# Interleaving the first w_in matmuls with the last x matmuls of batch 0 in a fused attention and feed-forward kernel

## The chip, the cores and the metric

One core of one Trainium2 chip. The time is the device time of one execution in microseconds (us). The unchanged kernel takes 279.9 us (median of 3 runs, 279.63 to 279.91; with three more runs, taken for the result, the median is 279.63).

## The reference

```python
q_s = softmax(q, axis=-1)              # q, k, v: 8 batches, 8 heads, 576 rows, 64 columns
k_s = softmax(k, axis=2)
kv  = einsum('bhsd,bhse->bhde', k_s, v)
x   = einsum('bhsd,bhde->bhse', q_s, kv)   # then heads side by side: 4608 x 512
out = gelu(x @ w_in) @ w_out               # w_in 512 x 2048, w_out 2048 x 512
```

Below, "x of a pair" is x of two heads (128 of the 512 columns). x0 to x3 are the four pairs, and each is also one quarter of the contraction with w_in.

## The kernel before

TensorE works through the batches (512 of the 576 rows of each; the other 64 rows of all batches make a ninth round): kv, x, 64 w_in matmuls in 16 column tiles, and 64 w_out matmuls. Batch 0 is special, for nothing precedes it that could hide its waits. Its start (cuts marked with "..."):

```python
def kv_tiles(b):                       # PSUM for kv
    if b == 0:
        p = [psum_h.tile([128, 512], FP32, tag="h", name="kv")[:, 0:256] for i in range(2)]
        ps = psum_a.tile([128, 4, 256], FP32, tag="a2", name="kv")
        st[b]["kvall"] = ps[:, 0::2]
        p += [ps[:, 0, :], ps[:, 2, :]]
    ...
def kv_norm(b, half=None):             # reciprocal of a column, then a product, on VectorE
    ...
    elif b == 0 and half == 0:         # pairs 0 and 1: two times two instructions
        parts = [(st[b]["kv"][hp].unsqueeze(1), kvc[b][:, hp:hp + 1], 1) for hp in range(2)]
    elif b == 0:                       # pairs 2 and 3: two instructions for both
        parts = [(ps, kvc[b][:, 2:4], 2)]
...
kv_mm(0, 0)
kv_norm(0, 0)
tp_mm(0, 1)                            # transposes of q, second half
tp_evac(0, 1)
x_tile(0, 2, psum_a, "a")
x_mm(0, 0)                             # x0 and x1
x_evac(0, 0, "s")                      # "s": PSUM to SBUF on ScalarE; otherwise on VectorE
cast_wi_dm(0, wi[0], 0, nc.scalar)     # first piece of w_in (256 columns), first quarter
for dm in range(1, NDM):
    cast_wi_dm(0, wi[0], dm, nc.gpsimd)
kv_mm(0, 1)
kv_norm(0, 1)
x_evac(0, 1)
x_tile(0, 3, psum_h, "h")
x_mm(0, 1)                             # x2 and x3
x_evac(0, 2, "s")
x_evac(0, 3)
cast_wi(1, wi[1], "p")                 # second piece, on GpSimd
table(AF.Gelu)
...
h_phase(0, {0: [lambda: cast_wi(2, wi[2], "v")], ...}, groups={0: 2, 4: 4, 8: 4}, ...)
```

`groups={0: 2}` runs the first two tiles together: both tiles' matmuls on x0, then both on x1, on x2, on x3. This is eight matmuls; "the ninth" below is the first one of the third tile.

The softmax here doesn't subtract the row's maximum and nothing guards it: scores larger than these inputs give would overflow.

## Time and profile before

| | us |
|---|---|
| time, median of 3 | 279.9 |
| span in the profile | 278.0 |
| TensorE busy | 270.0 |
| longest wait of TensorE after its start | 0.61, at 13.4 us |
| first w_in matmul, ninth, first w_out matmul | 14.32, 16.06, 28.15 |

The profile's lines are in the prediction. A line of a timeline gives start, length, engine, line of the program, operation, tiles, shapes and count; in square brackets stands the idle time before it and what ended it. The kernel is bound by TensorE from about 10 us on; until then TensorE runs warm-up matmuls on zeros (8.55 of the first 10 us, counted as busy) while data arrive. A change at the start can gain or lose only by moving the moment from which TensorE runs without waits.

### The profile page before, as it was taken

The numbers are of one execution on the slowest core, as the hardware profiler recorded it, in microseconds if no ns is written. First come the engines' busy times: TensorE is split into PE (matmuls) and PEld (weight loads), VectorE is DVE, ScalarE is ACT, GpSimd is POOL, SyncE is SP. The second block draws the span as 40 slices with busy tenths as digits, with TensorE's granted clock in tenths as the row PEclk, the third lists the DMA queues.
The fourth block names the chain that finished last, engine by engine and source line by source line (L and its number), as shares of the span: only waits on it lengthen the run. The fifth ranks groups of instructions, "written<-read, shape, count | busy, mean of one in ns | idle before, by whom it ended". The sixth has DMA issues, their size and how long they took to land.

```text
span 278.0 us, 4534 instructions
## 1 busy us (share of the span) xinstructions
PE 270.0 (97%) x1891; PEld 126.5 (46%) x1919; DVE 100.7 (36%) x153; ACT 158.0 (57%) x247; POOL 32.8 (12%) x26
## 2 busy tenths in 40 slices
PE   7899999999999999999999999999999999999995
PEld 3444454444444444444444444444444444444443
DVE  2876574319743540093008400651015200130012
ACT  4867675789377816791569246943683363136400
POOL 1520051002020220014000500050005000000000
PEclk9999999999999999999999999999999999999999
DMA  7999999963993139702981199017502500220033
GB/s 253 398 386 429 397 402 407 398 257 103 287 348 61 66 79 295 283 38 86 267 329 40 42 247 383 38 51 190 115 0 75 151 2 0 75 78 0 0 78 77
DMA packets 44980, 50.10 MB, mean 180 GB/s; under 512 B 20384, under 2 KB 29856, under 8 KB 44704
## 3 DMA queue, kind: packets, MB, share of 16 engines
q1 hardware_dynamic: 44560, 49.39, 53.5%
q10 hardware_dynamic: 400, 0.43, 0.6%
q8 instruction: 15, 0.25, 0.3%
q14 instruction: 5, 0.04, 0.0%
HBM read 36.70 MB, written 9.44 MB: 166 GB/s over the span
## 4 chain that ended last, share of the span: by engine, by line
PE 94%; DMA 2%; issue 1%; ACT 1%; SPq 1%; DVE 0%
PE ps L327 44%; PE ps L355 43%; DMA f<-in_k_dram 2%; PE kv L199 2%; PE ps L294 2%; PE ps L380 1%; PE pair L327 1%; ACT ek L150 0%; ACT v_aug L160 0%; PE ps L255 0%; SPq L90 0%; PE ps L299 0%; SPq L103 0%; PE tp L255 0%; DVE kvc L218 0%
## 5 line engine op out<-in xcount | busy, mean ns | idle before, releaser
L327 PE MATMUL ps<-xT,wi_bf 128*128 128x512 bf16 x557 | 124.2, 380 | 0.5
L355 PE MATMUL ps<-wo_bf,g 128*128 128x512 bf16 x543 | 122.1, 380 | 1.6 <-issue 1.1
L333 ACT ACTIVATE g<-ps 128x512 bf16<-128x512 f32 x142 | 83.5, 598 | 66.8 <-PE ps L327 66.8
L327 PEld LDWEIGHTS <-wi_bf 128*128 128x128 bf16 x576 | 56.1, 98 | 68.0 <-issue 0.5
L355 PEld LDWEIGHTS <-g 128*128 128x128 bf16 x560 | 53.9, 98 | 64.3 <-issue 0.4
L363 DVE COPY y_sb<-ps 128x512 f32<-128x512 f32 x33 | 22.7, 687 | 81.7 <-PE ps L355 78.6
L238 POOL TENSOR_TENSOR e<-e,recq 128x2048 bf16<-128x2048 bf16 (+1 forms) x9 | 25.7, 2855 | 176.2 <-DVE recq L237 141.5
L162 DVE CAST v_aug<-f 128x576 bf16<-128x576 f32 x24 | 16.4, 746 | 47.5 <-DMA f<-in_v_dram 47.5
L236 DVE TENSOR_REDUCE qsum<-e 128x16 f32<-128x1024 bf16 (+1 forms) x13 | 21.1, 1621 | 14.4 <-ACT e L145 14.3
L320 ACT CAST xT<-ps 128x512 bf16<-128x512 f32 x18 | 9.9, 588 | 28.8 <-PE ps L294 18.8
L145 ACT ACTIVATE e<-f 128x512 bf16<-128x512 f32 (+1 forms) x42 | 20.5, 556 | 3.5 <-DMA f<-in_q_dram 3.5
L150 ACT ACTIVATE ek<-f 128x2304 bf16<-128x2304 f32 (+1 forms) x10 | 17.2, 1728 | 0.5 <-DMA f<-in_k_dram 0.4
L318 DVE CAST xT<-ps 128x512 bf16<-128x512 f32 x17 | 11.0, 686 | 17.0 <-PE ps L294 14.1
L79 ACT ACT_TABLE_LOAD x9 | 11.5, 1283 | 2.8 <-issue 2.6
L475 PE MATMUL ps<-zeros 128*128 128x512 f32 (+1 forms) x15 | 9.2, 773 | 1.5 <-DVE zeros L500 1.5
L145 ACT ACT_TABLE_LOAD x7 | 9.0, 1283 | 0.1
L431 DVE CAST wi_bf<-w 128x512 bf16<-128x512 f32 x12 | 7.3, 654 | 2.2 <-DMA w<-in_moe_w_in_dram 1.9
L199 PEld LDWEIGHTS <-ek 64*64 64x64 bf16 x576 | 6.6, 105 | 2.6 <-ACT wo_bf L470 0.4
L199 PE MATMUL kv<-v_aug,ek 64*64 64x65 bf16 x576 | 7.2, 194 | 0.2 <-ACT v_aug L160 0.2
L294 PE MATMUL ps<-qT,kvc 64*64 64x512 bf16 x62 | 5.7, 391 | 0.8 <-DVE kvc L218 0.6
L238 DVE TENSOR_TENSOR e<-e,recq 128x1024 bf16<-128x1024 bf16 x4 | 6.2, 1546 | 0.1
L475 PEld LDWEIGHTS ps<-zeros 128*128 128x128 f32 x14 | 3.5, 260 | 6.0 <-issue 4.5
(39 smaller groups left out, 49.9 us busy)
## 6 DMA issues: line engine op xcount, KB each, us to landing
out_dram<-y_sb SPq DMA_DIRECT2D x32, 256.0 KB, 2.4
f<-in_k_dram SPq DMA_DIRECT2D x6, 1152.0 KB, 9.7
f<-in_v_dram SPq DMA_DIRECT2D x6, 1152.0 KB, 11.7
f<-in_q_dram SPq DMA_DIRECT2D x6, 1024.0 KB, 7.2
w<-in_moe_w_in_dram SPq DMA_DIRECT2D x6, 512.0 KB, 8.7
f<-in_v_dram SPq DMA_DIRECT2D x8, 288.0 KB, 6.8
f<-in_q_dram SPq DMA_DIRECT2D x4, 512.0 KB, 12.5
w<-in_moe_w_out_dram SPq DMA_DIRECT2D x2, 1024.0 KB, 11.7
```

Of the source, the lines that this page charges most:

```text
L79: nc.scalar.activation(out=scr[:, 1:2], in_=scr[:, 0:1], func=func)
L145: nc.scalar.activation(out=dst[:, i], in_=src[:, u], func=AF.Exp)
L150: nc.scalar.activation(out=ek[b % 2][:, i:i + n], in_=st[b]["kf"][:, i:i + n].rearrange("p x (n d) -> p x n d", n=NS), func=AF.Exp,)
L162: eng.tensor_copy(out=o, in_=i)
L199: nc.tensor.matmul(st[b]["kv"][hp][c, 0:D + 1], ek[b % 2][pr, hp, n, :], v_aug[b % 2][pr, hp, n, 0:D + 1], start=(n == 0), stop=(n == NS - 1),
L236: nc.vector.reduce_sum(out=qsum, in_=eq[:, :, hs, :], axis=AX.X)
L238: eng.tensor_tensor(out=eq[:, :, hs, :], in0=eq[:, :, hs, :], in1=recq.unsqueeze(3).to_broadcast([128, J, w, D]), op=ALU.mult,)
L327: nc.tensor.matmul(ps, wi_bf[:, dm, t * 128:(t + 1) * 128], st[c]["xT"][:, dm, :], start=(dm == 0), stop=(dm == NDM - 1),)
L333: nc.scalar.activation(out=st[c]["g"][:, t, :], in_=ps, func=AF.Gelu)
L355: nc.tensor.matmul(ps, st[c]["g"][:, t, j * 128:(j + 1) * 128], wo_bf[:, t, :], start=(t == 0), stop=(t == NDF - 1),)
L363: nc.vector.tensor_copy(out=y_sb, in_=ps)
L475: nc.tensor.matmul(ps, z[:, 0:128], z, start=True, stop=True)
```

## The change

The intent: TensorE idles 0.61 us while VectorE normalizes kv of pairs 2 and 3. Two w_in matmuls on x0 are to fill that hole. For this, x0 and its w_in quarter have to be there in time. So the normalization of pairs 0 and 1 is joined, x1 goes to ScalarE, and the whole first w_in piece is cast on GpSimd. In return that of pairs 2 and 3 is split. The core of the diff (kv_tiles and kv_norm only exchange the roles of the halves):

```diff
-        elif b == 0 and half == 0:
-            parts = [(st[b]["kv"][hp].unsqueeze(1), kvc[b][:, hp:hp + 1], 1) for hp in range(2)]
+        elif b == 0 and half == 1:
+            parts = [(st[b]["kv"][hp].unsqueeze(1), kvc[b][:, hp:hp + 1], 1) for hp in (2, 3)]
         elif b == 0:
-            parts = [(ps, kvc[b][:, 2:4], 2)]
+            parts = [(ps[:, 0::2], kvc[b][:, 0:2], 2)]
...
     x_evac(0, 0, "s")
-    cast_wi_dm(0, wi[0], 0, nc.scalar)
-    for dm in range(1, NDM):
+    x_evac(0, 1, "s")
+    for dm in range(NDM):
         cast_wi_dm(0, wi[0], dm, nc.gpsimd)
     kv_mm(0, 1)
     kv_norm(0, 1)
-    x_evac(0, 1)
+    h_begin(0)
+    hps = [psum_h.tile([128, M], FP32, tag="h", name="ps"),
+           psum_a.tile([128, 2, M], FP32, tag="a2", name="ps")[:, 0]]
+    for t in range(2):
+        h_mm(0, hps[t], t, (0,))
     x_tile(0, 3, psum_h, "h")
     x_mm(0, 1)
-    x_evac(0, 2, "s")
-    x_evac(0, 3)
+    x_evac(0, 2)
+    x_evac(0, 3, "s")
     cast_wi(1, wi[1], "p")
     table(AF.Gelu)
+    for dm in (1, 2, 3):
+        for t in range(2):
+            h_mm(0, hps[t], t, (dm,))
```

More of the change, by code (lines that the diff above doesn't have):

```diff
@@ L166, in cast_v_all, with kv_tiles @@
             cast_v(b, hp)
-    def kv_tiles(b):
-        if b == 0:
+    def kv_tiles(b, half):
+        if b == 0 and half == 1:
             p = [psum_h.tile([128, 512], FP32, tag="h", name="kv")[:, 0:256] for i in range(2)]
-            ps = psum_a.tile([128, 4, 256], FP32, tag="a2", name="kv")
-            st[b]["kvall"] = ps[:, 0::2]
-            p += [ps[:, 0, :], ps[:, 2, :]]
-        else:
+            st[b]["kv"] += p
+        elif "kv" not in st[b]:
             ps = psum_a.tile([128, 4, 256], FP32, tag="a2", name="kv")
             st[b]["kvall"] = ps
-            p = [ps[:, i, :] for i in place]
-        st[b]["kv"] = p
+            st[b]["kv"] = [ps[:, 0, :], ps[:, 2, :]] if b == 0 else [ps[:, i, :] for i in place]
     place = [1, 2, 0, 3]
@@ L188, in kv_mm @@
     def kv_mm(b, half):
-        if "kv" not in st[b]:
-            kv_tiles(b)
+        kv_tiles(b, half)
         for n in range(NS):
@@ L438, in cast_wi_dm @@
         w = w[:, dm, 0:n].rearrange("p (m c) -> p c m", c=r)
-        if eng is nc.scalar:
-            eng.copy(out=o, in_=w)
-        else:
-            eng.tensor_copy(out=o, in_=w)
+        eng.tensor_copy(out=o, in_=w)
     def load_wo(i):
@@ L519 @@
     x_tile(0, 1, psum_y, "y")
+    x_tile(0, 2, psum_a, "a")
     kv_mm(0, 0)
@@ L523 @@
     tp_evac(0, 1)
-    x_tile(0, 2, psum_a, "a")
     x_mm(0, 0)
     x_evac(0, 0, "s")
-    cast_wi_dm(0, wi[0], 0, nc.scalar)
-    for dm in range(1, NDM):
+    x_evac(0, 1, "s")
+    for dm in range(NDM):
         cast_wi_dm(0, wi[0], dm, nc.gpsimd)
@@ L531 @@
     kv_norm(0, 1)
-    x_evac(0, 1)
+    h_begin(0)
[3 more added lines that the diff above has]
+        h_mm(0, hps[t], t, (0,))
     x_tile(0, 3, psum_h, "h")
     x_mm(0, 1)
-    x_evac(0, 2, "s")
-    x_evac(0, 3)
+    x_evac(0, 2)
+    x_evac(0, 3, "s")
     cast_wi(1, wi[1], "p")
     table(AF.Gelu)
+    for dm in (1, 2, 3):
+        for t in range(2):
+            h_mm(0, hps[t], t, (dm,))
+    for t in range(2):
+        h_gelu(0, hps[t], t)
+    cast_wi(2, wi[2], "v")
     def ybank():
@@ L550 @@
     h_phase(0, {
-        0: [lambda: cast_wi(2, wi[2], "v")],
         2: [lambda: cast_wi(3, wi[3], "v")],
@@ L555 @@
         12: [lambda: cast_wo(1, wo[1])],
-    }, groups={0: 2, 4: 4, 8: 4}, banks={
+    }, t1=2, groups={4: 4, 8: 4}, banks={
         3: ybank, 6: ybank, 8: ybank,
```

## The prediction

> **What bounds the kernel now.** I read the busy times first, then the same figures stretch by stretch, then the start of the chain that ended last, then the order of instructions on each engine between 10 and 17 us, where the change lies.
>
> ```profile
> PE 270.0 (97%) x1891; PEld 126.5 (46%) x1919; DVE 100.7 (36%) x153; ACT 158.0 (57%) x247; POOL 32.8 (12%) x26
> ...
> 10.00:13.40 3.40, 3.16 (x94) 2.12 (x93) 2.27 (x6) 2.49 (x5) 1.42 (x3) 1.00 1.07 390
> 13.40:14.30 0.90, 0.32 (x4) 0.11 (x4) 0.83 (x3) 0.60 (x2) 0.90 (x3) 1.00 1.18 368
> 14.30:28.15 13.85, 13.75 (x67) 6.25 (x66) 9.43 (x15) 9.83 (x18) 1.36 (x3) 1.00 1.04 412
> 28.15:278.00 249.85, 244.22 (x1719) 114.47 (x1743) 83.74 (x121) 139.09 (x214) 26.50 (x12) 1.00 0.50 159
> ```
>
> TensorE (first figure after the length) is the bound. From 14.30 us on it has no wait worth the name, so a shift of its first w_in matmul reaches the end nearly undiminished, and whatever happens before counts only through that. The one hole in reach of the change is in 13.40:14.30, where it works 0.32 of 0.90 us:
>
> ```profile
> 13.43 0.18 DVE rec L217
> 13.61 0.02 issue
> 13.64 0.30 DVE kvc L218
> 13.94 0.04 issue
> 13.98 0.41 PE ps L294 x4
> ```
>
> This is the chain of waits: kv of head pairs 2 and 3 is done at 13.36, VectorE normalizes it until 13.93, x of those pairs starts at 13.98. That idle stretch of 0.61 us (the longest wait of TensorE after its start) is the most that the change can gain: 0.2% of 279.9 us. A result outside 2% is out of reach by this path.
>
> The timelines of TensorE, VectorE, ScalarE and GpSimd around it:
>
> ```profile
> 12.32 0.74 PE L294 MATMUL ps<-qT,kvc 64*64 64x512 bf16 x4
> 12.66 0.70 PE L199 MATMUL kv<-v_aug,ek 64*64 64x65 bf16 x36
> 13.98 0.41 PE L294 MATMUL ps<-qT,kvc 64*64 64x512 bf16 x4 [0.61 <-DVE kvc L218]
> 14.32 7.51 PE L327 MATMUL ps<-xT,wi_bf 128*128 128x512 bf16 x33
> ...
> 13.85 1.32 DVE L318 CAST xT<-ps 128x512 bf16<-128x512 f32 x2
> ...
> 13.10 0.59 ACT L320 CAST xT<-ps 128x512 bf16<-128x512 f32 x1 [0.91 <-PE ps L294]
> 13.58 0.42 ACT L440 CAST wi_bf<-w 128x256 bf16<-128x256 f32 x1
> 14.44 0.58 ACT L320 CAST xT<-ps 128x512 bf16<-128x512 f32 x1 [0.44 <-PE ps L294]
> ...
> 13.31 0.41 POOL L442 CAST wi_bf<-w 128x256 bf16<-128x256 f32 x1 [0.75 <-DMA w<-in_moe_w_in_dram]
> ```
>
> To see here: w_in's first piece reaches SBUF only at about 13.25 (GpSimd sat idle for its DMA), so no w_in matmul can run before 13.31 plus a cast. From 14.32 the eight matmuls of the first two tiles follow each other 0.216 us apart without a stall (one record is missing): the two of x0 and the two of x1 last until 15.2 and cover the evacuation of x2 (ACT, until 15.02) and x3 (DVE, until 15.16). The ninth starts at 14.32 + 0.01 + 8 x 0.216 = 16.06.
>
> **What the Trainium skill says.** "TensorE: Matmul & The Clock Gate", Back-to-back issue gap: N/2.4 + 2.5 ns, 216 ns at N = 512, for isolated matmuls. The trace agrees (0.216 us start to start). The same page, Part 3, The mechanism: weight loads overlap matmuls in flight only when the row group differs. Here a change of shape costs something: at 45 us this kernel already goes from two pieces of w_in matmuls (four, of which three were recorded) to x and back,
>
> ```profile
> 44.16 0.81 PE L327 MATMUL ps<-xT,wi_bf 128*128 128x512 bf16 x3
> 45.11 0.40 PE L294 MATMUL ps<-qT,kvc 64*64 64x512 bf16 x1
> 45.45 0.82 PE L327 MATMUL ps<-xT,wi_bf 128*128 128x512 bf16 x3
> ```
>
> 44.16 + 4 x 0.216 = 45.02, but x starts at 45.11: a switch to x costs 0.09 beyond a matmul. From x back, 0.34 pass instead of 0.216: 0.12 more. This fits the page, though the trace does not prove that the row group is the reason. "SBUF — State Buffer", Who interferes with whom: a VectorE cast in a two-port mode and GpSimd block each other. The trace shows the first VectorE cast of w_in, begun at 15.32 while GpSimd was casting until 15.89, at 1.04 us against 0.62 for the next. "ScalarE: Activation LUTs", What ACT_TABLE_LOAD costs: back-to-back activations overlap by about 93 ns. The trace: two gelus of 0.58 us start 0.48 apart.
>
> **The change part by part.** I walk the instruction order of the changed kernel with these durations. A result reaches TensorE about 0.06 us after its producer ends (VectorE 12.26, TensorE 12.32).
>
> 1. Normalization of pairs 0 and 1 joined, that of pairs 2 and 3 split. Joined: reciprocal at 11.84, 0.17; product 0.29 after a 0.03 gap: done 12.33, and all four x matmuls start at 12.39 (before: one at 12.32, three at 12.65). A gain of 0.26 for what follows.
> 2. kv of pairs 2 and 3 then waits for the last v cast on GpSimd (11.90 + 0.67 = 12.57, so 12.63). Its main stretch took 0.47 before (12.89 to 13.36): done at 13.10, against 13.36.
> 3. The split gives this back: the two separate pairs of instructions took 11.84 to 12.59 = 0.75 against 0.50 for a joined one. From 13.17: 13.92, so x of pair 3 could start at 13.98, exactly as before.
> 4. New first in line after kv: two w_in matmuls on x0. x0 is evacuated in time (12.39 + 0.45 + 0.59 = 13.43). But the cast of the first w_in quarter moved from ACT to GpSimd's first place: 13.31 + 0.41 = 13.72, usable 13.78. So TensorE idles 13.10 to 13.78 = 0.68: the hole isn't filled but moved ahead of the first w_in matmul.
> 5. Two w_in matmuls at 13.78 and 14.00. Then x of pairs 2 and 3 with one switch: 14.00 + 0.31 = 14.31 (13.98 before: 0.33 later). Back to w_in: 14.31 + 0.34 = 14.65; two matmuls on x1 (ACT finishes x1 at about 13.9, GpSimd the second quarter at 14.08), end of their slots at 15.09.
> 6. x2 and x3 come out later: VectorE takes x2 at 14.31 + 0.47 = 14.78, and 0.69 later it is done at 15.47; usable 15.54 (ACT has x3 by 15.35). Before, four matmuls covered this evacuation; now only two do, and TensorE stalls 15.09 to 15.54 = 0.45.
> 7. The last four of the eight start at 15.54, and the ninth at 15.54 + 0.01 + 4 x 0.216 = 16.41.
>
> Sum: 16.41 - 16.06 = 0.35 us later. Checked the other way, as idle time between 13.10 and the ninth: now 0.68 + 0.45 + switches 0.09 + 0.12, before 0.61 + 0.12, and kv 0.26 earlier: 1.34 - 0.73 - 0.26 = 0.35.
>
> What lies beside and costs nothing: GpSimd has one more cast of 0.41, so the second w_in tile group (two casts of 0.64) is done near 16.0 instead of 15.89; its first half is needed at 16.41, its second at 16.84. ACT loses a cast of 0.42 and gains an evacuation of 0.59; the gelu table load begins at 15.35 instead of 15.04 and the first gelu near 16.75 instead of 16.44. Its PSUM bank is wanted again at 16.41 + 8 x 0.216 = 18.14; no wait. VectorE's w_in casts start about 15.5 and end as GpSimd lets them, well before their use at 18.1. The DMA queue's order is unchanged.
>
> **The rivals.** (a) The intended gain: the two matmuls fill the hole and all that follows is up to 0.43 us earlier, 279.5. For it: kv ends 0.26 earlier and the second product no longer needs to gate w_in. Against: it needs w_in at 13.2, and the DMA brings it at 13.25 before any cast; and it needs x2 evacuated within two matmuls. If the piece landed 0.4 earlier, x would start at 13.98, and the ninth at 16.08: still no gain. (b) The stalls overlap less badly (x2 comes out faster, or the shape switches hide): a tie, 279.9 to 280.0. (c) w_in lands later than in this one profile, or GpSimd, casting next to VectorE, is slower: each 0.1 us is 0.1 us on the end, because the first cast has lost the 0.6 us of slack it had; 280.5 to 280.7. (d) The 0.35 is absorbed later at a DMA-bound spot: TensorE's other waits after 14.3 us sum to 1.1 us of issue in eight pieces or fewer and none is on a DMA, so I expect no absorption.
>
> **Range and chances.** 279.9 + 0.35 = 280.25; I say 280.2, pulled slightly to the ties. Three runs of before spread 0.3 us, and the DMA's landing adds as much: 279.7 to 280.7. To leave 2% takes 5.6 us, ten times anything moved here: 0.99 for the same.
>
> **What would show it.** In the changed profile: x of the first pairs as four at 12.39; kv over near 13.1; TensorE idle until about 13.78 with GpSimd's w_in cast as releaser; x again at 14.31; a second stall near 15.1 to 15.5 released by VectorE's cast of x2; the ninth w_in matmul at 16.4; and the first w_out matmul at 28.50 instead of 28.15. I am wrong if there is no second stall, or if the first w_in matmul runs before 13.6.

## The result, and the profile after

279.95 us (median of 6 runs, 279.85 to 280.33) against 279.63 us (6 runs of before, 279.6 to 279.91): ratio 1.0011, 95% interval 0.9998 to 1.0024, so the same within 2%. A ratio is the mean time of one kernel's fast runs over that of the other's of the same rounds, so not quite the ratio of these medians. The prediction's 280.2 is 0.25 us above the median, inside its range.

The stretches of the changed kernel, in the columns of those of before (length, then busy time and count of TensorE, weight loads, VectorE, ScalarE, GpSimd):

```profile
13.40:14.30 0.90, 0.62 (x5) 0.23 (x6) 0.52 (x3) 0.55 (x2) 0.90 (x4) 1.00 1.07 335
14.30:28.15 13.85, 13.55 (x64) 5.81 (x62) 8.98 (x14) 9.68 (x18) 1.41 (x3) 1.00 1.03 406
```

TensorE works 0.30 us more than before in the first stretch and 0.20 us less in the second: the hole was filled in part, and new ones came after it. (A few matmul records are missing, so such sums are rough: in the first stretch one of the two w_in matmuls on x0, in the second of before one of the first eight.) The holes are to be seen in the timelines of TensorE, GpSimd, ScalarE and VectorE:

```profile
12.42 0.41 PE L290 MATMUL ps<-qT,kvc 64*64 64x512 bf16 x4
12.66 0.51 PE L195 MATMUL kv<-v_aug,ek 64*64 64x65 bf16 x36
13.54 0.39 PE L323 MATMUL ps<-xT,wi_bf 128*128 128x512 bf16 x1 [0.36 <-POOL wi_bf L435]
14.07 0.41 PE L290 MATMUL ps<-qT,kvc 64*64 64x512 bf16 x4
14.42 0.60 PE L323 MATMUL ps<-xT,wi_bf 128*128 128x512 bf16 x2
15.27 1.02 PE L323 MATMUL ps<-xT,wi_bf 128*128 128x512 bf16 x4 [0.25 <-DVE xT L314]
...
11.67 0.67 POOL L162 CAST v_aug<-f 128x576 bf16<-128x576 f32 x1
13.07 1.47 POOL L435 CAST wi_bf<-w 128x256 bf16<-128x256 f32 x4 [0.74 <-DMA w<-in_moe_w_in_dram]
...
12.88 1.07 ACT L316 CAST xT<-ps 128x512 bf16<-128x512 f32 x2 [0.65 <-PE ps L290]
...
13.76 0.22 DVE L214 TENSOR_TENSOR kvc<-kv,rec 128x64 bf16<-128x64 f32 x1
14.53 0.69 DVE L314 CAST xT<-ps 128x512 bf16<-128x512 f32 x1 [0.55 <-PE ps L290]
```

What to see: all four x matmuls of the first pairs start at once (12.42), kv ends at 13.17, and TensorE then waits for GpSimd's cast, which waited for its DMA. The first w_in matmul on x0 stands at 13.54, the record of the second is missing (x comes 0.54 later, which is room for two). x2 and x3 follow at 14.07, later than before (13.98). Here w_in was not alone on the path: ScalarE had x0 ready at 13.46, just before GpSimd's cast (13.48), and the split normalization, whose last product is done at 13.98 and usable at about 14.04, would have held x back nearly as long. Two matmuls on x1 follow, then a second wait, for VectorE's evacuation of x2. (The bracket says 0.25 because the modelled end of the earlier matmul lies late; from start to start it is 0.63 us where 0.216 would do, so 0.41 are lost.) The ninth starts at 16.13, 0.07 later than before.

The first w_out matmul is 0.27 later, at 28.41. Most of the rest was lost at one place, where a weight load waited for VectorE's cast of the last w_in piece:

```profile
25.59 0.33 PEld L323 LDWEIGHTS <-wi_bf 128*128 128x128 bf16 x3 [0.43 <-DVE wi_bf L427]
```

The matmul after it came 0.38 us after its predecessor, 0.16 too late. Its piece of w_in landed at 24.36, against 23.49 in the trace of before.

### The profile page after: what moved, and what is told of

It is laid out like the page before. It is cut to its first block, busy times and chain, and to the rows that moved or that the text cites. A ratio compares the mean times of both kernels' runs of the same rounds, so it can differ in the third digit from the quotient of the medians.

```text
span 278.3 us, 4538 instructions
## 1 busy us (share of the span) xinstructions
PE 270.3 (97%) x1891; PEld 126.3 (45%) x1919; DVE 100.0 (36%) x152; ACT 158.3 (57%) x247; POOL 33.1 (12%) x27
## 4 chain that ended last, share of the span: by engine, by line
PE 97%; issue 1%; DVE 1%
PE ps L323 44%; PE ps L351 43%; PE ps L468 3%; PE kv L195 2%; PE ps L290 2%; PE ps L376 1%; PE pair L323 1%; PE ps L251 0%; DVE kvc L214 0%; DVE xT L314 0%; PE ps L295 0%; DVE zeros L493 0%; PE tp L251 0%; DVE rec L213 0%; DVE y_sb L381 0%
## 5 line engine op out<-in xcount | busy, mean ns | idle before, releaser
L316 ACT CAST xT<-ps 128x512 bf16<-128x512 f32 x19 | 10.3, 588 | 28.2 <-PE ps L290 18.1
L314 DVE CAST xT<-ps 128x512 bf16<-128x512 f32 x16 | 10.4, 686 | 17.5 <-PE ps L290 14.7
L461 DVE CAST wo_bf<-w 128x2048 bf16<-128x2048 f32 (+1 forms) x4 | 4.4, 1090 | 3.8 <-DMA w<-in_moe_w_out_dram 3.8
```

## The experiments

Each was timed in 5 rounds. The intervals are about 0.0013 wide on either side (0.36 us), more than most differences here, so times alone separate little. The traces do more. In all twelve of them the span ends 249.81 to 249.92 us after the first w_out matmul: what happens before it goes into the time in full. Two moments vary by chance from trace to trace. One is the start of the first kv normalization: followed back from it, the chain leads over ScalarE's casts and exponentials to the landing of k (before, after_again) or of q (before_again), and in the first trace of the changed kernel to TensorE's warm-up matmuls. The other is the landing of w_in's first piece. So I give those two, what follows from them, and the time from the first normalization to the first w_out matmul (last column but one).

| kernel | first norm. | w_in lands | kv over | x2, x3 | first w_in matmul | ninth | first w_out | norm. to w_out | ratio to before |
|---|---|---|---|---|---|---|---|---|---|
| before | 11.84 | 13.26 | 13.37 | 13.98 | 14.32 | 16.06 | 28.15 | 16.31 | |
| before_again | 11.60 | 13.02 | 13.13 | 13.74 | 14.09 | 15.82 | 27.91 | 16.31 | 1.0005 |
| changed | 11.87 | 13.02 | 13.17 | 14.07 | 13.54 | 16.13 | 28.41 | 16.54 | 1.0011 |
| after_again | 11.63 | 12.97 | 12.93 | 14.03 | 13.49 | 16.09 | 28.18 | 16.55 | 1.0014 |
| h_behind_x | 11.69 | 13.02 | 12.98 | 13.85 | 14.19 | 15.93 | 28.01 | 16.33 | 1.0006 |
| halves | 11.65 | 13.02 | 12.96 | 14.07 | 13.54 | 16.27 | 28.42 | 16.77 | 1.0023 |
| swap_evac | 11.78 | 12.98 | 13.08 | 14.03 | 13.49 | 15.98 | 28.07 | 16.29 | 1.0005 |
| w_two | 11.69 | 12.44 | 12.99 | 13.85 | 13.33 | 15.91 | 28.00 | 16.31 | 0.9994 |
| act_cast | 11.73 | 13.04 | 13.03 | 14.22 | 13.69 | 16.28 | 28.37 | 16.64 | 1.0019 |
| join_last | 11.96 | 13.32 | 13.52 | 14.38 | 13.86 | 16.44 | 28.53 | 16.56 | 1.0014 |
| join_both | 11.60 | 12.94 | 12.90 | 13.51 | 13.86 | 15.59 | 27.68 | 16.08 | 0.9993 |
| join_both_w | 11.79 | 12.85 | 13.09 | 13.71 | 14.05 | 15.79 | 27.88 | 16.09 | 0.9992 |

In the "x2, x3" column stands when all four matmuls could run; h_behind_x could begin x2 at 13.52. The time from the first normalization to w_out compares kernels fairly only where kv sets the path. Where TensorE waits for w_in, a late normalization makes it smaller: swap_evac's 16.29 is 0.26 below after_again's 16.55, but its normalization was 0.15 later at the same landing, so 0.11 is the change's.

**before_again**: no edit.

> The kernel before, unchanged, run as an experiment: what repeats and what the DMA moves by chance. Theory (TensorE's start sets the end; the changed kernel's two stalls outweigh its earlier kv): ratio 1.000 within 0.001, ninth w_in matmul at 16.0 to 16.1 us, first w_out matmul at 28.15 to 28.2. Rival (the 0.3 us between the two kernels is only chance of the DMA): a trace of the unchanged kernel would show a stall of TensorE between 17 and 28 us behind a late cast of the last w_in piece, and times as much apart as the two kernels are.

The ratio was 1.0005 (0.9992 to 1.0018). DMAs landed 0.24 us earlier than in the first trace of before, and everything shifted along with them; the first w_out matmul came at 27.91. On TensorE:

```profile
13.74 0.41 PE L294 MATMUL ps<-qT,kvc 64*64 64x512 bf16 x4 [0.61 <-DVE kvc L218]
14.09 2.12 PE L327 MATMUL ps<-xT,wi_bf 128*128 128x512 bf16 x8
```

The hole is the same 0.61 us, and there is no stall before 28 us. So the absolute moments differ by a quarter of a microsecond from trace to trace, but the time from the first normalization to w_out repeats: 16.31 both times. The expectations of 16.0 to 16.1 for the ninth and 28.15 to 28.2 for w_out were wrong for this reason.

**after_again**: no edit.

> The changed kernel, unchanged. Theory: ratio 1.001 (0.3 us), ninth w_in matmul at 16.1 to 16.4 depending on when the first w_in piece lands (about 13.0 or 13.25), stall of about 0.4 us before the fifth w_in matmul behind VectorE's cast of x2. In the first trace 0.17 us more were lost at 25.6 us, behind the cast of the last w_in piece, which landed 0.87 us later than before. If that lateness is the change's doing it comes back here; if it is chance it does not, or it appears in other kernels as well.

The ratio was 1.0014 (1.0002 to 1.0027).

```profile
13.49 0.39 PE L323 MATMUL ps<-xT,wi_bf 128*128 128x512 bf16 x1 [0.56 <-DVE rec L213]
14.03 0.41 PE L290 MATMUL ps<-qT,kvc 64*64 64x512 bf16 x4
15.23 1.02 PE L323 MATMUL ps<-xT,wi_bf 128*128 128x512 bf16 x4 [0.25 <-DVE xT L314]
```

The stall before the fifth w_in matmul came back (0.63 from start to start), the one at 25.6 us did not: the last w_in piece landed at 23.12, and its lateness in the first trace was chance. This time the first normalization started nearly as in before_again (11.63 against 11.60), kv was over at 12.93, and TensorE idled 0.56 us until the cast of w_in. (The profile names VectorE as the releaser, whose reciprocal ended last by its records; the program waits there for GpSimd's cast, which ended at 13.43, for x0, and for a VectorE copy that was long done.) With w_in landing alike (12.97 and 13.02), the changed kernel's ninth matmul is 0.27 us later than that of before.

**h_behind_x**: the two matmuls on x0 back behind x2 and x3.

```diff
-    for t in range(2):
-        h_mm(0, hps[t], t, (0,))
     x_tile(0, 3, psum_h, "h")
     x_mm(0, 1)
+    for t in range(2):
+        h_mm(0, hps[t], t, (0,))
```

> Changed kernel with the two matmuls on x0 moved back behind x of the last two pairs; all else as changed. Theory: the stall before the fifth w_in matmul is gone (four matmuls of 0.216 us cover the evacuation of x2), in return TensorE idles 0.85 us between kv (13.17) and x (about 14.03); first w_in matmul at 14.37, ninth at 16.11, so a tie with the changed kernel (16.13) within 0.1 us and with before (16.06). Rival (the interleaving itself saves what it fills, and only the moved cast costs): ninth 0.2 to 0.4 us later than in the changed kernel.

```profile
13.52 0.74 PE L290 MATMUL ps<-qT,kvc 64*64 64x512 bf16 x4 [0.53 <-DVE kvc L214]
14.19 2.12 PE L323 MATMUL ps<-xT,wi_bf 128*128 128x512 bf16 x8
```

The second stall is gone, as expected: four matmuls cover x2's evacuation again. It wasn't a tie, though. The ninth came at 15.93, and the time from normalization to w_out is 16.33, 0.22 below after_again and equal to before. I had taken 14.03 for the start of x from the first changed trace, where kv was late; here the normalization allowed it at 13.85. So the interleaving itself costs about 0.2 us where kv is early, and the moved casts cost nothing once it is undone.

**halves**: x2 and x3 each evacuated by two engines at once (shortened; in the program it is a helper).

```diff
-    x_evac(0, 2)
-    x_evac(0, 3, "s")
+    for hp in (2, 3):
+        nc.vector.tensor_copy(out=xT[:, hp, 0:256], in_=ps[:, 0:256])
+        nc.scalar.copy(out=xT[:, hp, 256:512], in_=ps[:, 256:512])
```

> Changed kernel, but x2 and x3 each evacuated half by VectorE and half by ScalarE, x2 first. Theory (the second stall, 0.41 us, is the evacuation of x2 by one engine, 0.69 us): x2 is ready about 0.25 to 0.3 us earlier, the stall falls to 0.1 to 0.2 us, the ninth w_in matmul starts 0.25 us earlier (15.9), before that of the kernel before; end 0.25 us earlier than the changed kernel unless TensorE then waits for the last w_in piece near 25.5. Rival (the stall has another cause, the weight load or GpSimd's cast): stall stays 0.4 us and ninth at 16.1.

It was worse: ratio 1.0023 (1.0009 to 1.0037), ninth at 16.27, stall 0.55 instead of 0.41 us. VectorE and ScalarE:

```profile
14.53 0.76 DVE L321 CAST xT<-ps 128x256 bf16<-128x256 f32 x2 [0.76 <-PE ps L290]
...
14.99 0.70 ACT L322 CAST xT<-ps 128x256 bf16<-128x256 f32 x2 [1.25 <-DVE xT L321]
```

ScalarE did not work beside VectorE but waited for it, twice: the halves are in one PSUM bank, and the program has a wait there. The Trainium skill's page "PSUM — Partial Sum Buffer", section PSUM bank collisions raise a hardware error, says that two engines must not access one bank and quadrant at once, reads included, and that a scheduler adds such a wait. The trace agrees with the wait (VectorE's first half ends at 14.95, ScalarE's starts at 14.99). My expectation overlooked it. For the question the run is a half answer: whatever delays x2 delays the fifth matmul, which again started when x2 was out. Another 0.07 us were lost at 18.7 us.

**swap_evac**: the same question without that flaw.

```diff
-    x_evac(0, 2)
-    x_evac(0, 3, "s")
+    x_evac(0, 2, "s")
+    x_evac(0, 3)
```

> Changed kernel, with x2 evacuated by ScalarE and x3 by VectorE instead of the other way round. This replaces the run with halves, where ScalarE was made to wait for VectorE at the same PSUM bank. Theory (the second stall is the time of x2's evacuation): ScalarE takes 0.59 us instead of 0.69 and begins 0.03 later, so the stall before the fifth w_in matmul falls from 0.41 (start to start 0.63) to about 0.34 (0.56), first to ninth w_in matmul 2.53 us instead of 2.60. Rival (something else ends the stall): 2.60 again. Too small for the times; the trace decides.

x2 on ScalarE, and the fifth w_in matmul on TensorE:

```profile
14.48 0.58 ACT L316 CAST xT<-ps 128x512 bf16<-128x512 f32 x1 [0.63 <-PE ps L290]
...
15.12 0.38 PE L323 MATMUL ps<-xT,wi_bf 128*128 128x512 bf16 x1
```

With x again at 14.03, the fifth matmul came at 15.12 instead of 15.23, and from the first to the ninth it took 2.49 us instead of 2.60. The stall fell from 0.41 to 0.30 us (0.34 expected). The second stall is the evacuation of x2.

**w_two**: the first w_in load in two DMAs.

```diff
-    wi_parts = [1, 1, 4, 2, 2]
+    wi_parts = [2, 1, 4, 2, 2]
```

> Changed kernel, with the load of the first w_in piece in two DMAs of two quarters each. Theory (the first stall of the changed kernel is the landing of this piece plus one cast, 12.97 + 0.46 in the last trace of it): the first half lands about 0.65 us earlier, GpSimd casts it from about 12.4, and the first w_in matmul is then gated by the evacuation of x0 alone (13.22 + 0.06 = 13.28 instead of 13.49); x of the last pairs at 13.8 instead of 14.03; the second stall stays at 0.4 us; ninth w_in matmul at about 15.9 instead of 16.09, end 0.2 us earlier than the changed kernel. Rival (kv or the split normalization of the last pairs holds the path): nothing moves, x at 14.03 and ninth at 16.09.

```profile
12.49 1.49 POOL L435 CAST wi_bf<-w 128x256 bf16<-128x256 f32 x4
...
13.33 0.59 PE L323 MATMUL ps<-xT,wi_bf 128*128 128x512 bf16 x2 [0.34 <-ACT xT L316]
13.85 0.41 PE L290 MATMUL ps<-qT,kvc 64*64 64x512 bf16 x4
15.05 1.24 PE L323 MATMUL ps<-xT,wi_bf 128*128 128x512 bf16 x5 [0.25 <-DVE xT L314]
```

As expected, though the half piece landed at 12.44 and not at about 12.3: the wait for GpSimd became a shorter one for ScalarE's x0, x moved to 13.85 and the ninth to 15.91. The ratio was 0.9994 (0.998 to 1.0007). The first stall was the landing plus one cast. With both loss terms known, the changed kernel plus this one number is as good as before, not better. Nor would a still earlier landing help: the split normalization of pairs 2 and 3 was done at 13.80 here, so x could not have started before about 13.85.

**act_cast**: the first quarter's cast back on ScalarE, between x0 and x1 (shortened).

```diff
+    nc.scalar.copy(out=<first quarter of wi_bf>, in_=<first quarter of w>)
     x_evac(0, 1, "s")
-    for dm in range(NDM):
+    for dm in range(1, NDM):
```

> Changed kernel, with the first quarter of w_in cast on ScalarE as before, after x0 and ahead of x1. Theory (the cast of this quarter stands on the path): ScalarE finishes x0 at about 13.2 to 13.3, casts until 13.65, first w_in matmul at 13.7 instead of 13.49, all after it 0.2 us later, ninth at 16.3. Rival (the cast is beside the path, the moved engine doesn't matter): ninth at 16.1 as in the changed kernel.

```profile
13.21 0.42 ACT L520 CAST wi_bf<-w 128x256 bf16<-128x256 f32 x1
...
13.69 0.61 PE L323 MATMUL ps<-xT,wi_bf 128*128 128x512 bf16 x2 [0.66 <-ACT wi_bf L520]
```

The ratio was 1.0019 (1.0006 to 1.0031), the ninth at 16.28. The cast stands on the path, and GpSimd was the better place for it, not because it is faster (0.41 against 0.42 us) but because it was free.

**join_last**: normalization as before (first two pairs split, last two joined), the rest as changed. Edit: the hunks of kv_tiles and kv_norm undone, both w_in tiles in psum_h, the third in psum_a.

> Changed kernel, with the normalization as before: the first two pairs split, the last two joined (and PSUM tiles handed out to suit). Theory (prediction's steps 1 to 3: the swap gives 0.26 us and takes it back; and x of the last pairs waits anyway for the two w_in matmuls ahead of it): kv over 0.2 us later than in the changed kernel, x of the last pairs still at 14.0 to 14.1, ninth at 16.1: a tie within 0.1 us. Rival (the swap is the costly part): x and the ninth move by 0.2 us or more, in either direction.

```profile
13.86 0.59 PE L326 MATMUL ps<-xT,wi_bf 128*128 128x512 bf16 x2 [0.34 <-ACT xT L319]
14.38 0.41 PE L293 MATMUL ps<-qT,kvc 64*64 64x512 bf16 x4
```

The absolute moments missed: this trace has the latest landing of w_in (13.32) and the latest first normalization (11.96) of all. Counted from the landing x starts 1.06 us later and the ninth 3.12 us later; in after_again it is 1.06 and 3.12. The time from normalization to w_out is 16.56 against 16.55, the ratio 1.0014 in both: a tie, as expected. But two things ended together ahead of the first w_in matmul: GpSimd's cast at 13.79, and at 13.81 ScalarE's evacuation of x0, which the bracket names. x0 is late because x of the first pairs runs in two steps again (12.44 and 12.78). So the tie holds for arrival times like these. For an early w_in the traces suggest otherwise: the first w_in matmul stands 1.90 us after the first normalization here, held by x0, and 1.64 in w_two. By this estimate the swap would be worth about 0.25 us there; that wasn't tested.

**join_both**: both normalizations joined, w_in behind x (shortened).

```diff
-        if b == 0 and half == 1:
-            p = [psum_h.tile(...)[:, 0:256] for i in range(2)]
-            st[b]["kv"] += p
-        elif "kv" not in st[b]:
+        if "kv" not in st[b]:
             ps = psum_a.tile([128, 4, 256], FP32, tag="a2", name="kv")
             st[b]["kvall"] = ps
-            st[b]["kv"] = [ps[:, 0, :], ps[:, 2, :]] if b == 0 else [...]
+            st[b]["kv"] = [ps[:, i, :] for i in ((0, 2, 1, 3) if b == 0 else place)]
...
+        elif b == 0:
+            parts = [(ps[:, half::2], kvc[b][:, 2 * half:2 * half + 2], 2)]
...     # and the w_in matmuls on x0 behind x_mm(0, 1); w_in tiles 0 and 1 in psum_h, tile 2 in psum_a
```

> A version that should beat both: kv of all four pairs in the four places of one two-bank PSUM tile, so that both normalizations are joined, and the w_in matmuls behind x of the last pairs. Theory: the gain of the joined first half is kept (kv over at 12.95), the joined second one takes 0.50 instead of 0.75, so x of the last pairs starts at about 13.55, the first w_in matmul at 13.9 and the ninth at 15.6 to 15.65, 0.45 us before the changed kernel and 0.2 before the kernel before; end 0.2 us below before, unless TensorE then meets the last w_in piece near 25 us. Rival (x0, x1 or w_in's casts hold the path once kv is early): first w_in matmul still at 14.1 to 14.2, no gain over before.

```profile
13.51 0.41 PE L285 MATMUL ps<-qT,kvc 64*64 64x512 bf16 x4 [0.62 <-DVE kvc L209]
13.86 2.33 PE L318 MATMUL ps<-xT,wi_bf 128*128 128x512 bf16 x10
```

The hole is still 0.6 us, but it starts and ends 0.23 us earlier, and no stall follows. The second half of kv can share banks with the first, because x of the first pairs, which stands between them on TensorE, has waited for the first normalization anyway. Ninth at 15.59, 279.44 us (279.35 to 279.89) against 279.67 (279.41 to 279.99): ratio 0.9993 (0.9981 to 1.0006).

**join_both_w**: the same with the two-part load of w_two.

> The version with both normalizations joined and w_in behind x, with the first w_in load in two DMAs as well. Theory (in that version w_in's first piece isn't on the path, it was cast at 13.40 and used at 13.86): a tie with it, first w_in matmul 0.96 us after the end of kv (12.90 to 13.86), no stall up to the ninth, ratio to before again 0.9993 within 0.0006. Rival (part of its gain was an early landing): a further gain of 0.2 us or more.

From the end of kv to the first w_in matmul 0.96 us, no stall, normalization to w_out 16.09, ratio 0.9992 (0.998 to 1.0005): a tie, so the gain is not a matter of the landing. Two kernels of this form reach w_out 0.22 us sooner than before by the trace. In times this is 0.2 us of 280; each interval holds 1, so the times alone don't prove it.

## Why the prediction was right

By its own steps, with the first changed trace and after_again:

1. The joined normalization let all four x matmuls start together: predicted 12.39, measured 12.42. Right.
2. kv over at 13.10: measured 13.17 with a first normalization 0.03 later, and 12.93 in after_again, 0.20 before that of before_again (predicted 0.26). The time is right, the reason given for it is not: kv did not wait for GpSimd's v cast, which ended at 12.34 in both traces. It started 0.24 after x (12.66 and 12.42), which the prediction's numbers happen to put at the same moment, and took 0.51 instead of 0.47.
3. The split gives it back: predicted done at 13.92 and x of pair 3 possible at 13.98; measured 13.98 and about 14.04 in the first trace, with kv 0.07 later. Right. The split normalization is thus a second limit on x, close behind the two w_in matmuls (14.07), and in w_two both were reached together (13.85). join_last, without the swap, ended in a tie, for w_in and x0 were late together; with w_in early the swap may be worth about 0.25 us (the estimate above).
4. The hole is moved ahead of the first w_in matmul, whose releaser is GpSimd's cast. Mechanism right (w_two, act_cast). The term was mis-sized: 0.68 predicted, 0.37 and 0.56 measured, since w_in landed at about 13.0 and not at 13.25 as in the one trace that I had. With that, one of the prediction's two signs of being wrong came true: the first w_in matmul ran before 13.6, at 13.54 and 13.49. The reason is the landing, so I read this sign as too strict.
5. One switch of shape more, ahead of x: first w_in matmul to x 0.53 predicted, 0.54 measured in both traces.
6. The second stall behind x2's evacuation: 0.45 predicted, 0.41 measured in both; swap_evac and h_behind_x show its cause.
7. Ninth 0.35 us later (and the first w_out matmul, 28.50 for 28.15): 0.07 in the first pair of traces, 0.27 in the second (w_out 0.27 in both). For the second pair the sum reads: hole 0.56 + stall 0.41 + switch 0.11 - hole before 0.61 - kv earlier 0.20 = 0.27. In the first it is 0.37 + 0.41 + 0.11 - 0.61 - 0.20 = 0.08. The changed trace of the first pair had its w_in 0.24 us earlier than the trace of before, the second pair had nearly equal landings.

Two things about the number are luck. The 280.2 rests on 279.9, the median of three runs, which lies 0.27 us above the median of six; the difference of the medians of six is 0.32 us, near the predicted 0.35, but no larger than the spread of the runs, and the interval of the first ratio holds 1 (that of after_again, 1.0002 to 1.0027, does not). And the prediction had not foreseen how the 0.3 us would come about in the first changed trace: only 0.07 at the ninth matmul, and most of the rest behind the last w_in piece. The cause of that late landing (24.36) is open. A stall there came back in none of the eleven other traces (latest landing 23.83), and the ratio came back (1.0014, after 1.0011; 0.3 to 0.4 us) in after_again, whose trace lacks it. Rival (a), the intended gain, is refuted by the traces: even with w_in early the ninth is at 15.91, no earlier from the first normalization than in before. Rival (b), a tie through a shorter stall or hidden switches, did not happen: stall and switch came out at 0.41 and 0.11. Rival (c), a later landing or a slower GpSimd, stays untested: in join_last w_in was late, but x0 was too. Rival (d), absorption later, did not happen: the span after the first w_out matmul is constant within 0.11 us.

One statement of the prediction was too narrow: that the 0.61 us are the most that the change can gain. The joined first normalization, a part of this change, gains by another way: before, x of the first pairs started in two steps (12.32 and 12.65), with it at once. join_both gains 0.22 us so, with the hole still at 0.62.

## What to carry to other kernels

Before you fill a hole with later work, ask when that work's own inputs arrive: here a DMA and a cast brought them only in the middle of the hole, so the filler waited instead. And count what the moved work covered in its old place: the two matmuls taken out from behind x2's evacuation left it bare, at 0.41 us. What did move the start of TensorE's run forward was to shorten the step ahead of the hole (the first normalization, joined instead of split): the hole stayed as long, but began and ended 0.23 us earlier.

## What the Trainium skill lacked or had wrong

- "TensorE: Matmul & The Clock Gate", Back-to-back issue gap: it gives about 131 ns per matmul as sustained for pairs of weight load and matmul at N = 512, and calls 216 ns the isolated gap. Here sustained pairs run 216 ns apart (0.215 to 0.217 us in the trace of before, once 0.227 just after x).
- No page gives a figure for a change of tile shape, neither this one nor "TensorEngine Tiling (Array Packing)", which speaks of changing the mode without a time. Here a switch from 128x128 to 64x64 weights cost 0.09 us beyond a matmul, and one back 0.12 us (first of x to first of w_in 0.34 instead of 0.216).
- "GPSIMD Engine Reference", section Elementwise — side-by-side cycle accounting, gives GpSimd as about two times slower than VectorE, for an addition of two tensors. For a cast to bf16 the page has no time (its table Engine selection only calls one-input operations roughly line-rate); here GpSimd took 0.64 us for 128x512 and VectorE 0.62, and for 128x256 GpSimd 0.41 and ScalarE 0.42.
- How far a landing moves from run to run is on none of the pages cited here. In these twelve traces the first w_in piece, where loaded whole, landed between 12.94 and 13.32 us, as much as the whole effect under study.
